# A new order of the start-up batch and of the unit stream in a fused attention and feed-forward kernel

## The chip, the cores and the metric

The kernel runs on one core of one Trainium2 chip. The metric is the device time in microseconds (us), taken as the median of several runs; most runs of a kernel agree within 0.3 us. Engines are named as the profile names them: PE is the matmul engine (TensorE), PEld its weight loads, DVE is VectorE, ACT is ScalarE, POOL is GpSimd, SP is SyncE. The profiled run also has a *span*, from its first to its last instruction, which is some 1.7 us shorter than the time of the same run.

## The reference

```python
# q, k, v: (8 batches, 8 heads, 576 positions, 64)
rel = pos[:, None] - pos[None, :]
mask_local   = (rel >= 0) & (rel < 32)                                 # heads 0..3
mask_strided = (rel >= 0) & (pos[None, :] % 32 == pos[:, None] % 32)   # heads 4..7
scores = where(mask, q @ k.T / sqrt(64), -1e9)
attn   = exp(scores - max) / (sum(exp(...)) + 1e-09)
x      = (attn @ v) as (8*576, 512)          # 4608 tokens
out    = relu(x @ w_in)**2 @ w_out           # 512 -> 2048 -> 512
```

## The kernel before

The attention is cut into *units*: unit u is batch u // 4 and head pair u % 4. Pairs 0 and 1 are local, pairs 2 and 3 strided. A unit goes through `step_T` (q or k transposed on PE into a PSUM bank, copied out by ACT for q and by DVE for k), `step_S` (scores on PE, exponentials on ACT, mask on DVE), `step_D` (outputs on PE, division by the row sum on DVE) and `step_E` (outputs transposed into `xt`, the input of the feed-forward part). Batch 0 has nothing to run beside and is written out by hand in `first_steps`; its strided units have `step_TS` for the transposes and `step_N`, `step_O` for row sums and outputs. The units from 8 on are spread between the feed-forward matmuls by `stream_steps` and `plan`.

The kernel takes eight PSUM banks (two, one and five), handed out in rotation from three lists:

```python
banks = {nm: [psum.tile([128, 512], FP32, name=f"{nm}{i}") for i in range(n)]
         for nm, n in (("ph", 2), ("py", 1), ("pt", 5))}
...
def step_T(u, name):
    ...
    pt = bank("ph" if u < 4 else "pt").bitcast(BF16)[:, 0:S]
    ...
    if name == "q":
        nc.scalar.copy(o, i)            # ACT
    else:
        nc.vector.tensor_copy(o, i)     # DVE
...
def step_TS(b, name, half, copy):       # header shortened here
    pt = bank("ph" if b == 0 else "pt").bitcast(BF16)[:, 0:S]
```

A *first-layer group* is 512 tokens by 128 of the 2048 columns: four matmuls of 512 columns, one for each head pair. Token chunk 0 lies within batch 0, so its groups can be fed piece by piece as each pair's `xt` comes in. `NP` groups are held open at once for that. Groups 0 and 1 take the two ph banks, group 2 the py bank, and groups from 3 on take pt banks *out of the rotation* until they are done:

```python
NP = 5
...
def part(kks, ffs=range(NP)):           # one of the four matmuls of each open group
    for ff in ffs:
        mm1(0, ff, kks, first_order, None if ff < 2 else "py" if ff == 2 else "pt")
...
order = [..., (o(2), 0), (lambda: part((a,)), 0), (E_(1), 0), (o(3), 0), (lambda: part((b,)), 0),
         (lambda: part((c,)), 0), (lambda: part((d,)), 0)]
# mm1: pool "pt" -> banks["pt"].pop(0); after the relu: banks["pt"].append(ph)
```

The number beside each step is how many filler matmuls follow it. They use no data; they keep PE busy while it would wait (18 matmuls of 512 columns in the profile, 7.5 us of its busy time). The constants (masks, and biases that add a large negative number to masked scores of batch 0) are built on DVE ahead of the first steps.

The softmax here doesn't subtract the row's maximum and nothing guards it: scores larger than these inputs give would overflow.

## Time and profile before

| | before |
|---|---|
| time, median of 3 runs | 310.63 us (310.61 to 311.06) |
| span of the profiled run | 309.1 us |
| PE busy | 301.5 us, 98% |
| PE busy in the first 20 us | 17.36 of 20 |
| PE busy in 70 to 80 us | 8.88 of 10 |
| mean granted clock | 1.00 |

PE is busy 98% of the time, so there is little to win: only the few stretches in which it is not full, or in which its instructions are stretched by short waits. A matmul of 512 columns stands in the trace as 0.379 us long, and the next one starts 0.216 after it (median of 985 such pairs in a row), so some 0.16 of a wait can pass without a gap (an estimate from these two figures). The prediction below shows the lines for this: the busy times, the stretches, and PE's waits. In a line of a timeline the columns are the start, the duration, the engine, the source line, the operation with output and input, their shapes, and how many instructions are joined in the line; in brackets is the idle time before it and what ended it.

### The profile page before, as it was taken

Reading aid. Unit: us, or ns where it says so; the run is one execution under the profiler, and the core shown is the slowest. Engines: PE = TensorE matmul, PEld = TensorE weight load, DVE = VectorE, ACT = ScalarE, POOL = GpSimd, SP = SyncE. Lnnn points to the kernel's source line nnn. Section 1 sums busy time; section 2 is a strip of 40 time slices with the busy share of each in tenths; the row PEclk is TensorE's granted clock in tenths of the full one; section 3 lists DMA queues with packets and bytes.
Section 4 is the critical chain, followed back from the end, with each engine's and each line's share of the span. In section 5 each row is a group of like instructions: output and inputs, shape, how many; then the busy total and the mean of one; then the engine's idle time right before and its main releaser. Section 6 shows DMA issues by size and latency. Waiting matters only on the chain.

```text
span 309.1 us, 6113 instructions
## 1 busy us (share of the span) xinstructions
PE 301.5 (98%) x2370; PEld 149.6 (48%) x2370; DVE 157.5 (51%) x408; ACT 165.0 (53%) x342; POOL 75.4 (24%) x103
## 2 busy tenths in 40 slices
PE   8999999998999999999999999999999999999995
PEld 3554564544554554445444544444444444444444
DVE  5366654578677884675566577445422222222200
ACT  3767737786566765554555655555444434344311
POOL 8653300540981045350461042000000000000000
PEclk9999999999999999999999999999999999999999
DMA  8999996997999899897999483221231000000121
GB/s 162 166 193 205 191 210 119 221 176 147 141 195 174 168 229 204 164 230 174 182 232 215 105 171 92 72 55 53 72 98 44 35 34 36 34 34 36 41 95 69
DMA packets 94119, 40.75 MB, mean 132 GB/s; under 512 B 78859, under 2 KB 87755, under 8 KB 93899
## 3 DMA queue, kind: packets, MB, share of 16 engines
q0 software_dynamic: 34528, 15.00, 39.1%
q1 hardware_dynamic: 59562, 25.37, 34.3%
q8 instruction: 18, 0.29, 0.4%
q14 instruction: 11, 0.08, 0.1%
HBM read 37.64 MB, written 13.57 MB: 166 GB/s over the span
## 4 chain that ended last, share of the span: by engine, by line
PE 93%; DVE 3%; ACT 1%; POOL 1%; issue 1%; ACTq 0%; POOLq 0%
PE ph L482 39%; PE py L518 28%; PE ph L518 9%; PE pt L337 4%; PE pt L422 4%; PE pt L482 1%; PE pt L288 1%; PE pt L518 1%; PE ph L504 1%; PE pt L458 1%; DVE kTl L303 1%; PE pt L325 1%; PE pt L398 1%; DVE x_l L435 1%; DVE x_s L435 1%
## 5 line engine op out<-in xcount | busy, mean ns | idle before, releaser
L482 PE MATMUL ph<-xt,w_in_b 128*128 128x512 bf16 x552 | 139.9, 379 | 0.0
L488 ACT ACTIVATE r<-ph 128x512 bf16<-128x512 f32 x138 | 82.4, 598 | 95.3 <-PE ph L482 93.0
L491 DVE TENSOR_TENSOR g_sb<-r 128x512 bf16<-128x512 bf16 x144 | 65.1, 453 | 105.8 <-ACT r L488 104.6
L518 PE MATMUL py<-w_out_b,g_sb 128*128 128x512 bf16 x400 | 102.8, 379 | 0.0
L482 PEld LDWEIGHTS <-w_in_b 128*128 128x128 bf16 x576 | 52.3, 98 | 55.3 <-issue 0.2
L518 PEld LDWEIGHTS <-g_sb 128*128 128x128 bf16 x560 | 50.8, 98 | 54.7 <-issue 0.4
L347 ACT ACTIVATE e<-pt 72x288 bf16<-72x288 f32 (+1 forms) x128 | 45.4, 407 | 12.7 <-PE pt L337 12.7
L518 PE MATMUL ph<-w_out_b,g_sb 128*128 128x512 bf16 x144 | 35.1, 379 | 0.0
L422 PEld LDWEIGHTS <-e 128*128 128x128 bf16 (+1 forms) x384 | 20.3, 97 | 15.3 <-issue 0.6
L435 DVE TENSOR_TENSOR x_s<-pt,rinv 72x384 bf16<-72x384 f32 (+1 forms) x36 | 18.3, 509 | 1.2
L434 DVE RECIPROCAL rinv<-pt 96x6 f32<-96x6 f32 (+2 forms) x68 | 12.6, 185 | 11.5 <-PE pt L422 11.1
L522 ACT COPY y<-py 128x512 f32<-128x512 f32 x25 | 14.6, 586 | 7.0 <-PE py L518 7.0
L435 DVE TENSOR_TENSOR x_l<-pt,rinv 96x384 bf16<-96x384 f32 x32 | 17.7, 554 | 1.1
L353 DVE TENSOR_TENSOR e<-e,mask_str 72x576 bf16<-72x576 bf16 x28 | 13.1, 482 | 3.8 <-ACT e L347 3.7
L353 DVE TENSOR_TENSOR e<-e,mask_full 128x576 bf16<-128x576 bf16 x28 | 12.6, 449 | 2.4 <-ACT e L347 2.2
L220 POOL CAST vl<-vl_st 128x768 bf16<-128x768 f32 x6 | 5.7, 951 | 32.7 <-DMA vl_st<-in_v_dram 20.1
L422 PE MATMUL pt<-vs,e 72*128 72x65 bf16 x192 | 11.9, 193 | 0.8 <-DVE e L353 0.4
L140 POOL CAST q_l<-q_st 96x768 bf16<-96x768 f32 x6 | 5.4, 900 | 25.9 <-DVE x_l L435 15.6
L522 ACT COPY y<-ph 128x512 f32<-128x512 f32 x9 | 5.3, 584 | 10.9 <-PE ph L518 10.9
L422 PE MATMUL pt<-vl,e 128*128 128x65 bf16 x192 | 10.9, 193 | 0.0
L612 POOL DMA_DIRECT2D vs<-in_v_dram x12 | 9.8, 819 | 0.2 <-issue 0.2
L337 PEld LDWEIGHTS <-kT_s 64*72 64x72 bf16 x256 | 5.9, 113 | 7.0 <-issue 6.2
(104 smaller groups left out, 197.5 us busy)
## 6 DMA issues: line engine op xcount, KB each, us to landing
out_dram<-y SPq DMA_DIRECT2D x35, 256.0 KB, 2.6
w_out_b<-in_moe_w_out_dram POOLq DMA_DIRECT2D x4, 512.0 KB, 15.4
q_d<-in_q_dram POOLq DMA_DIRECT2D x6, 288.0 KB, 7.4
k_d<-in_k_dram POOLq DMA_DIRECT2D x6, 288.0 KB, 8.5
q_st<-in_q_dram SPq DMA_DIRECT2D x12, 144.0 KB, 4.7
k_st<-in_k_dram SPq DMA_DIRECT2D x12, 144.0 KB, 4.5
vl_st<-in_v_dram SPq DMA_DIRECT2D x12, 144.0 KB, 4.1
v_st<-in_v_dram SPq DMA_DIRECT2D x6, 288.0 KB
```

The lines of the kernel that those rows point to most:

```text
L337: nc.tensor.matmul(pss[row][half][0:kn, w * i:w * (i + 1)], lhsT, rhs, start=u > 3, stop=True, skip_group_check=u < 4)
L347: nc.scalar.activation(e[0:kn, lo:lo + S // 2], pss[row][half][0:kn, 0:S // 2], AF.Exp, scale=scale)
L353: nc.vector.tensor_tensor(x, x, m, op=ALU.mult)
L422: nc.tensor.matmul(po[:, n - n0, :], e[0:kn, pos(n):pos(n) + 128], rhs[0:kn, src(n), 0:D + 1], start=True, stop=True)
L434: nc.vector.reciprocal(rinv[0:w, 0:m], po[0:w, 0:m, D:D + 1])
L435: nc.vector.tensor_tensor(x, po[0:w, 0:m, 0:D], rinv[0:w, 0:m].to_broadcast([w, m, D]), op=ALU.mult)
L482: nc.tensor.matmul(ph, w_in_b[:, kk, 128 * ff:128 * (ff + 1)], xt[kk][:, 512 * c:512 * (c + 1)], start=(kk == order[0]), stop=(kk == order ...
L488: nc.scalar.activation(r, ph, AF.Relu)
L491: later(1, lambda: nc.vector.tensor_tensor(g[:, ff, :], r, r, op=ALU.mult))
L518: nc.tensor.matmul(py, g[:, ff, 128 * j:128 * (j + 1)], w_out_b[:, ff, :], start=(ff == 0), stop=(ff == 15))
L522: nc.scalar.copy(y, py)
L612: nc.gpsimd.dma_start(out=t[:, NJ * i:NJ * (i + 1), 0:D], in_=v[b, h + i].rearrange("(p j) d -> p j d", j=NJ))
```

## The change

The intent is to take waits from PE in two places. In batch 0 the scores of unit 1 come before the strided transposes and unit 0's outputs before unit 3's scores, six groups are open instead of five, and two mask constants are built after the first casts. In the stream, k is transposed a step earlier than q instead of after it, and each unit's q and k are cast to bf16 as a pair, which takes k's cast a group earlier, and both casts of batch 4 a group earlier still. The q casts of batches 3 and 4 go to ACT.

```diff
-    NP = 5
+    NP = 6
...
         order = [(t(0, "q"), 2), (t(0, "k"), 2), (cast1("q"), 0), (cast1("k"), 0), (S_(0), 0),
-                 (t(1, "q"), 0), (t(1, "k"), 1), (ts("q", 0, v_), 0), (ts("q", 1, v_), 0), (S_(1), 1),
-                 (ts("k", 0, v_), 0), (ts("k", 1, s_), 1), (S_(2), 0), (S_(3), 0),
-                 (D_(0, 0), 0), (D_(0, 1), 1), (n(2), 1), (E_(0), 0), (D_(1, 0), 1), (n(3), 0), (D_(1, 1), 0),
+                 (t(1, "q"), 0), (t(1, "k"), 1), (S_(1), 0), (ts("q", 0, v_), 0), (ts("q", 1, v_), 1),
+                 (ts("k", 0, v_), 0), (ts("k", 1, s_), 1), (S_(2), 0), (D_(0, 0), 0), (D_(0, 1), 0), (S_(3), 0),
+                 (n(2), 1), (D_(1, 0), 0), (E_(0), 0), (n(3), 0), (D_(1, 1), 0),
                  (o(2), 0), (lambda: part((a,)), 0), (E_(1), 0), (o(3), 0), (lambda: part((b,)), 0),
...                                                   # stream_steps, per unit u
             if u < hi:
                 order.append(D_(u, 0))
+                if more:                              # u + 2 is local and has transposes on PE
+                    order.append(T_(u + 2, "k"))
             if u > lo:
                 order.append(E_(u - 1))
             if u < hi:
-                if u + 2 < hi and has_T(u + 2):
+                if more:
                     order.append(T_(u + 2, "q"))
                 order.append(D_(u, 1))
-                if u + 2 < hi and has_T(u + 2):
-                    order.append(T_(u + 2, "k"))
...                                                   # constants
+    cast_qk_local(0, (nc.scalar.copy, nc.vector.tensor_copy))      # (this line stood here before)
     nc.vector.tensor_copy(mask_full, ...)             # these three moved from ahead of the
     nc.vector.memset(mask_full[0:32, 0], 0.0)         # casts of unit 0 to behind them
     nc.vector.tensor_scalar(bias_s, ...)
...                                                   # plan
-                at(g1 + 2 * i, lambda u=4 * b + i: cast_qk_local(u, dve2, "q"))
-                at(g1 + 2 * i + 1, lambda u=4 * b + i: cast_qk_local(u, dve2, "k"))
+                copies = dve2 if b == 2 else (nc.scalar.copy, nc.vector.tensor_copy)
+                at(g1 + 2 * i, lambda u=4 * b + i, c=copies: cast_qk_local(u, c))
-    plan(4, 64, 62)
+    plan(4, 64, 61)
```

More of the change, by code (lines that the diff above doesn't have):

```diff
@@ L568, in stream_steps @@
         for u in range(lo, hi + 1):
+            more = u + 2 < hi and has_T(u + 2)
             if u < hi - 1:
@@ L663 @@
     nc.vector.memset(bias_l[0:32, 0, 0], -NEG)
-    nc.vector.tensor_copy(mask_full, mask_loc.to_broadcast([128, NL, QL]))
-    nc.vector.memset(mask_full[0:32, 0], 0.0)
-    nc.vector.tensor_scalar(bias_s, mask_str.to_broadcast([SP_, NJ // 2, SP_]),
-                            NEG, -NEG, op0=ALU.mult, op1=ALU.add)
     load_qk_str(0, "k", room=w_out_b[:, 4:10, :])
@@ L686 @@
     cast_qk_local(0, (nc.scalar.copy, nc.vector.tensor_copy))
+    nc.vector.tensor_copy(mask_full, mask_loc.to_broadcast([128, NL, QL]))
+    nc.vector.memset(mask_full[0:32, 0], 0.0)
+    nc.vector.tensor_scalar(bias_s, mask_str.to_broadcast([SP_, NJ // 2, SP_]),
+                            NEG, -NEG, op0=ALU.mult, op1=ALU.add)
     for fn, spare in first:
```

## The prediction

> **What bounds the kernel now.** I read the page's busy times and chain first, then stretches of 10 us, then what TensorE (PE) waited for, and last the order in time around each wait. From the page (busy times, then the chain that ended last):
>
> ```profile
> PE 301.5 (98%) x2370; PEld 149.6 (48%) x2370; DVE 157.5 (51%) x408; ACT 165.0 (53%) x342; POOL 75.4 (24%) x103
> ...
> PE 93%; DVE 3%; ACT 1%; POOL 1%; issue 1%; ACTq 0%; POOLq 0%
> ```
>
> PE is the bound nearly everywhere, so a reordering wins only what PE loses in waits. Where that is (stretch, its length, then busy us of PE, PEld, DVE, ACT, POOL):
>
> ```profile
> 0.00:10.00 10.00, 8.08 (x53) 3.39 (x54) 5.11 (x21) 4.56 (x8) 8.69 (x19) 1.00 0.94 157
> 10.00:20.00 10.00, 9.28 (x143) 5.58 (x143) 4.51 (x13) 8.00 (x21) 5.21 (x8) 1.00 1.37 181
> ...
> 70.00:80.00 10.00, 8.88 (x105) 4.97 (x101) 8.25 (x24) 5.36 (x14) 3.11 (x5) 1.00 0.63 114
> 80.00:90.00 10.00, 9.71 (x121) 5.60 (x121) 6.23 (x18) 5.97 (x16) 8.72 (x12) 1.00 1.70 199
> 90.00:100.00 10.00, 9.73 (x103) 5.03 (x102) 7.77 (x22) 6.19 (x15) 3.68 (x6) 1.00 1.83 178
> ```
>
> All other stretches of 20 to 300 us show PE full. So there are two places: the first 20 us (batch 0) and 70 to 95 us (the stream, units 10 to 16). The waits of PE, in order of time:
>
> ```profile
> 10.10 0.67 PE L189 MATMUL ph<-ident,w_out_b 96*128 96x96 bf16 x12 [0.52 <-ACT qT L301]
> 17.45 0.43 PE L458 MATMUL pt<-ident,x_l 96*128 96x96 bf16 x6 [0.55 <-DVE x_l L435]
> ...
> 74.89 0.22 PE L422 MATMUL pt<-vs,e 72*128 72x65 bf16 x2 [0.41 <-DVE x_l L435]
> 75.53 0.30 PE L422 MATMUL pt<-vs,e 72*128 72x65 bf16 x4 [0.42 <-DVE e L353]
> 79.54 0.43 PE L337 MATMUL pt<-qT,kTl 64*128 64x96 bf16 x12 [0.29 <-DVE kTl L303]
> 85.09 0.43 PE L337 MATMUL pt<-qT,kTl 64*128 64x96 bf16 x12 [0.29 <-DVE kTl L303]
> 93.27 0.43 PE L288 MATMUL pt<-ident,q_l 96*128 96x96 bf16 x6 [0.27 <-DVE q_l L140]
> ```
>
> [...] a "busy" PE hides waits of up to some 0.2 us; I therefore measure losses between starts. [...] in the trace the first-layer matmuls start at 19.24, 19.47, 19.69, 19.90, about 0.22 apart. [...] nothing of PE's starts between 74.01+0.47 and 74.89. [...]the trace shows 0.83 us for the one such cast on ACT (at 3.99), against 0.35 us for a bf16 one on DVE. I use 0.8.
>
> **The change, part by part.** All sums are between starts. The words "two PSUM banks for the last outputs" name nothing in the diff: the last outputs already alternate between the two ph banks, and I give that nothing.
>
> *Stream, 70 to 95 us.* What is lost now, against the same steps without a wait:
> - Scores of unit 12 (79.54) and 13 (85.09) come 0.58 after a four-matmul step that elsewhere takes 0.12 (106.09 to 106.21): 0.46 each. The cause is k's transpose coming right before: its DVE copy takes 0.74. The change puts k's transpose some 2 us earlier, so the copy is done. Gain 0.92. What is left is q's copy on ACT (0.64, possibly behind a 0.59 output copy); I have it end just when the scores come up, so 0 to 0.1 lost again.
> - q's transpose of unit 16 (93.27) comes 1.30 after a four-matmul group that takes 0.87: 0.43, because the cast sat late in DVE's queue (92.87). The casts now come a group earlier, q's on ACT, and k's transpose, not q's, is first. Gain 0.43.
> - Scores of unit 11 plus the first outputs of unit 10 took 1.66 (74.01 to 75.67); the like pair at 88.78 took 0.59. Lost: 1.07. DVE had four casts of 0.35 in the 4 us before; two go to ACT. DVE then frees the bank near 74.5 instead of 74.84 and finishes the mask near 74.9 instead of 75.48. But two casts of 0.8 now stand between ACT's exponentials, the last of unit 10 ends near 74.3 instead of 73.39, and in the new bank rotation unit 11's scores want that bank: some 0.35 of new wait before 74.01+. I have the pair end near 75.1: gain 0.55.
>
> Sum: 0.92 + 0.43 + 0.55 = 1.9, less 0.15 for the small ACT waits: 1.75 gained.
>
> *Batch 0.* I carried the new order on by hand with the durations and latencies of the trace.
> - k's cast goes ahead of the mask constants on DVE: it can start at 5.25, not 5.83. Two warm-up matmuls of 0.42 hold PE to 6.18, so k's transpose moves from 6.43 to 6.18: gain 0.25 so far.
> - Unit 1's scores go ahead of the strided q's transposes. The latter waited at 9.20 to 10.10; now the scores wait for their own k copy, to 9.97 (before: scores from 10.95). ACT's exponentials start 1.0 earlier. But the four strided transposes now follow each other through two ph banks: q half 0 at 10.79, DVE copies of 0.46 and 0.38, then k half 1 not before 12.19, its copy on ACT 12.66 to 13.30, scores of unit 2 at 13.35 instead of 13.39. The gain is nearly gone.
> - Unit 0's outputs come before unit 3's scores (14.17 instead of 15.46), so the 0.55 wait at 17.45 goes. In exchange unit 3's second half waits for the bank of the first output (x_l done 15.41) and the row sums for the second (16.12). Together with two warm-ups fewer (0.43) the first part of the six groups starts near 19.0 instead of 19.24.
> - Six groups open leave two pt banks in rotation. Unit 1's transposed output takes pt0, unit 3's two halves pt1 and then pt0 again, so the second half must wait for ACT's copy out of pt0. Before, the three had three banks and PE ran through:
>
> ```profile
> 20.33 0.42 PE L458 MATMUL pt<-ident,x_l 96*128 96x96 bf16 x6
> 20.68 0.50 PEld L398 LDWEIGHTS <-g_sb 72*64 72x64 bf16 x16
> 20.68 0.62 PE L398 MATMUL pt<-e,g_sb 72*64 72x72 bf16 x16
> 20.79 0.64 ACT L464 COPY xt<-pt 128x576 bf16<-128x576 bf16 x1 [0.80 <-PE pt L458]
> ```
>
> The copy ends 21.43 - 20.33 = 1.10 after the transposes start; PE has 0.5 of work before the second half needs the bank. New wait: 0.6. After: first part 19.0 to 20.3 (six of 0.216), transposes 20.3, second half of unit 3 at 21.45, three more parts of 1.3 from 21.67 to 25.57. Before, the same six groups were done at 24.48 (five) + 0.86 = 25.34.
>
> So batch 0 costs 0.2 net: about 1.0 of waits and fillers removed, 1.2 of bank waits added. I trust this to 0.6 either way; ten small waits are in it.
>
> *Elsewhere.* Casting batch 2 in pairs on DVE and the shifted ph banks (first group of chunk 1 on the other bank) meet a PE without waits; nothing. The two kernels have the same matmuls but for two warm-ups, so PE's work is the same.
>
> Sum: -1.75 + 0.2 = -1.55 in the span; 310.63 - 1.55 = 309.1.
>
> **The rivals.**
> 1. *The bank wait of the six groups is worse, or its gain better.* For worse: two banks must serve three tiles, and each bank wait is ACT or DVE time on PE's path. Against: the sixth group's 0.22 is filler exactly where unit 1's copy is awaited. If the wait after the first part vanished, 308.5; if batch 0 lost 0.8 instead of 0.2, 309.7.
> 2. *ACT becomes the bound of 70 to 80 us.* For: the two casts are 1.6 us of new ACT work in some 4 us in which it already has 3.5 us to do, in order, and relus free the first-layer banks. Against: ACT is busy 5.36 of 10 there, with 0.98 idle just before unit 11's exponentials. If the whole 1.07 stayed, 309.1 + 0.55 = 309.7; if the casts also delayed the relus by 0.5, 310.2.
> 3. *Transfers take over.* A kernel that runs 1.5 us earlier meets loads that don't move. The v rows of batch 3 land at 83.91 and 84.34 and are used at 86.33; batch 0's v at 13.68, used at 15.46 before and at 14.17 by my reckoning; the four w_in parts land at 16.33 to 20.97, used from 19.0 to 24.3. All have at least 0.5 left. If one bound, it would give back up to 1: 310.1.
> 4. *Nothing moves*, the stream's gain being hidden by later waits. From 95 us on PE never waits, with the casts' chain gone from batch 5 on, so earlier work stays earlier unless transposing transfers bind. 310.6.
>
> **Range and chances.** The centre is 309.1. Batch 0 gives +-0.6, the stream +-0.6, later transfers up to +0.7, runs differ by 0.45 (310.61 to 311.06). That makes 308.1 to 310.4. Faster by 2% would take 6.2 us; the whole kernel has only some 2.4 us of waits in the stream and about as much again in batch 0 after the first load. Slower by 2% would take a new wait of a size that nothing here suggests. So 0.01 each, 0.98 within 2%.
>
> **What would show it.** After: no wait of PE on kTl at the two score groups near 79 and 84; none on q_l near 92; a wait of the scores of unit 11 on ACT's e near 74, with two casts among ACT's exponentials; a wait of PE on ACT's xt copy (L464) of about 0.6 between the first and second part of the six groups; the scores of unit 2 still near 13.4; the sixth group done near 25.6. Wrong would be: waits of PE on a transfer, batch 0 ending more than 0.8 away from that, or ACT's casts holding first-layer groups.

## The result, and the profile after

Beside each other on one chip, the kernel before took 310.93 us (median of 6 runs, 310.61 to 311.37) and the changed kernel 309.86 us (6 runs, 309.78 to 310.65). The ratio is 0.9968, with a 95% interval of 0.9954 to 0.9982. Here and below a ratio is the mean time of one kernel's fast runs over that of the other's of the same rounds, so it is not quite the ratio of the medians. The change is a gain of about 1.0 us. The spans of the profiled runs are 309.1 and 308.1.

The page of the changed kernel, busy times and the chain that ended last:

```profile
PE 300.7 (98%) x2368; PEld 149.9 (49%) x2368; DVE 157.0 (51%) x404; ACT 167.3 (54%) x346; POOL 75.3 (24%) x103
...
PE 91%; DVE 5%; ACT 2%; POOL 1%; issue 1%; ACTq 0%; POOLq 0%
```

Nothing has changed hands: PE is still the bound. The four instructions that ACT has more, and DVE less, are the casts that went there. The stretches of the changed kernel, with the same columns as in the prediction (the last three are PE's granted clock and two measures of the transfers):

```profile
0.00:10.00 10.00, 7.65 (x55) 3.32 (x55) 5.76 (x21) 4.59 (x8) 8.69 (x19) 1.00 1.00 162
10.00:20.00 10.00, 9.14 (x140) 5.70 (x141) 5.20 (x14) 7.70 (x21) 5.89 (x9) 1.00 1.34 190
20.00:30.00 10.00, 9.52 (x63) 4.61 (x62) 5.56 (x21) 5.86 (x12) 4.04 (x6) 1.00 1.26 205
...
70.00:80.00 10.00, 9.65 (x116) 5.54 (x116) 8.20 (x23) 7.43 (x19) 2.60 (x4) 1.00 0.59 120
...
90.00:100.00 10.00, 9.91 (x103) 5.25 (x102) 7.66 (x20) 7.57 (x17) 4.34 (x6) 1.00 1.72 155
```

The stream has filled up: 9.65 instead of 8.88 in 70 to 80 us, 9.91 instead of 9.73 in 90 to 100. The start has not. PE's 20 to 30 us, which were full before (10.00), now have a hole of 0.48 us, and 70 to 80 us still lacks 0.35.

**The stream.** PE's lines around the score steps of units 11 to 14, and two of DVE's, from the timeline of the changed kernel:

```profile
74.34 0.49 PE L337 MATMUL pt<-qT_s,kT_s 64*72 64x72 bf16 x16
75.04 0.67 PE L422 MATMUL pt<-vs,e 72*128 72x65 bf16 x6 [0.20 <-DVE x_l L435]
75.54 1.03 PE L518 MATMUL ph<-w_out_b,g_sb 128*128 128x512 bf16 x4
...
79.05 0.43 PE L337 MATMUL pt<-qT,kTl 64*128 64x96 bf16 x12
...
90.48 0.34 DVE L140 COPY k_l<-k_st 96x768 bf16<-96x768 bf16 x1
90.53 0.47 PE L337 MATMUL pt<-qT_s,kT_s 64*72 64x72 bf16 x16
90.75 0.45 DVE L353 TENSOR_TENSOR e<-e,mask_str 72x576 bf16<-72x576 bf16 x1
90.93 0.62 PE L422 MATMUL pt<-vs,e 72*128 72x65 bf16 x6
91.39 1.03 PE L518 MATMUL ph<-w_out_b,g_sb 128*128 128x512 bf16 x4
...
92.25 0.42 PE L288 MATMUL pt<-ident,k_l 96*128 96x96 bf16 x6
```

Subtract starts to read it, because a start of the next work counts every wait, shown or hidden. In the kernel before, the wait at 93.27 has a bracket of 0.27, and between starts it costs 0.43 (four matmuls before it take 1.30, elsewhere 0.87):

| part of the stream | before | after | difference |
|---|---|---|---|
| unit 11's scores to the end of unit 10's first outputs (74.34 to 75.54) | 1.66 | 1.20 | -0.46 |
| from there to unit 12's scores (75.54 to 79.05) | 3.87 | 3.51 | -0.36 |
| the same stretch before unit 13's scores, which start at 84.24 | 5.55 | 5.19 | -0.36 |
| four matmuls to unit 16's first transpose (91.39 to 92.25) | 1.30 | 0.86 | -0.44 |
| unit 15's scores and unit 14's outputs (90.53 to 91.39) | 0.59 | 0.86 | +0.27 |
| sum | | | -1.35 |

The first four are waits that the change removed: those on kTl at 79.54 and 85.09 and on q_l at 93.27 no longer stand in the trace. The last is a new one. PE's outputs at 90.93 need the mask that DVE applies at 90.75, and DVE now does the cast at 90.48 right before it. The line shows no bracket, since the wait lies inside the group of six: 0.62 long, where six such matmuls without a wait end within about 0.35.

**Batch 0.** Four lines at the start, from the timeline of the kernel before and then from that of the changed kernel:

```profile
5.17 0.47 DVE L664 COPY mask_full<-mask_loc 128x576 bf16<-128x576 bf16 x1
5.52 1.66 POOL L237 DMA_DIRECT2D vl<-in_v_dram  x1
5.83 0.55 DVE L140 CAST k_l<-k_st 96x768 bf16<-96x768 f32 x1
7.05 0.76 DVE L303 COPY kTl<-ph 128x576 bf16<-128x576 bf16 x1 [0.67 <-PE ph L288]
```

```profile
5.17 0.71 DVE L140 CAST k_l<-k_st 96x768 bf16<-96x768 f32 x1
5.52 1.21 POOL L237 DMA_DIRECT2D vl<-in_v_dram  x1
5.80 1.03 DVE L684 COPY mask_full<-mask_loc 128x576 bf16<-128x576 bf16 x1
7.02 0.75 DVE L303 COPY kTl<-ph 128x576 bf16<-128x576 bf16 x1
```

The cast of k moved forward, from 5.83 to 5.17, and the transposes that need it from 6.43 to 5.94. But the copy of the mask, now behind the cast, took 1.03 us instead of the 0.47 of before, and kTl's copy queues behind it on DVE. It begins at 7.02; before it began at 7.05. Then the end of batch 0, from the timeline:

```profile
20.39 0.42 PE L458 MATMUL pt<-ident,x_l 96*128 96x96 bf16 x6
20.75 0.32 PE L398 MATMUL pt<-e,g_sb 72*64 72x72 bf16 x8
...
21.54 0.32 PE L398 MATMUL pt<-e,g_sb 72*64 72x72 bf16 x8 [0.48 <-ACT xt L464]
21.80 0.61 PE L482 MATMUL ph<-xt,w_in_b 128*128 128x512 bf16 x2
```

Before, the sixteen matmuls of unit 3's output ran in one go from 20.68 and the second part of the groups began at 21.23, 0.90 after the transposes. Now the second eight wait for ACT to read unit 1's transposed output out of the bank that they need, and the second part begins 1.41 after the transposes. All six groups are done at 25.69; before they were done at 25.34.

So the change gave 1.36 in the stream and lost 0.35 in batch 0: together 1.0, which is the difference of the spans.

### The profile page after: what moved, and what is told of

Same layout as the page of the kernel before. It is cut to its first block, busy times and chain, and to the rows that moved or that the text cites.

```text
span 308.1 us, 6114 instructions
## 1 busy us (share of the span) xinstructions
PE 300.7 (98%) x2368; PEld 149.9 (49%) x2368; DVE 157.0 (51%) x404; ACT 167.3 (54%) x346; POOL 75.3 (24%) x103
## 4 chain that ended last, share of the span: by engine, by line
PE 91%; DVE 5%; ACT 2%; POOL 1%; issue 1%; ACTq 0%; POOLq 0%
PE ph L482 37%; PE py L518 28%; PE ph L518 9%; PE pt L337 4%; PE pt L422 4%; PE pt L482 2%; PE pt L288 1%; DVE x_l L435 1%; PE pt L518 1%; PE ph L504 1%; PE pt L458 1%; DVE e L353 1%; DVE g_sb L491 1%; DVE k_l L140 0%; DVE kTl L303 0%
## 5 line engine op out<-in xcount | busy, mean ns | idle before, releaser
L220 POOL CAST vl<-vl_st 128x768 bf16<-128x768 f32 x6 | 5.0, 828 | 37.5 <-PE ph L482 21.2
L140 POOL CAST q_l<-q_st 96x768 bf16<-96x768 f32 x6 | 6.6, 1107 | 19.0 <-ACT r L488 16.5
```

## The experiments

Account A, which the trace above tells, says three things. The stream's gain comes from k's earlier transposes together with the casts. Batch 0 loses to the sixth group's bank and gains nothing at its start, because the mask constants now stand where they hold kTl's copy. And each of these losses can be repaired alone. Against it stand three rivals: that a part of the difference is only scatter between runs, that the transfers of v would take back what is repaired, and, in the stream, that the casts alone or the order alone do everything.

The unit of account below is a *shift*: how much later ACT's relus and output copies start than the same ones of the kernel before, counted in order. Over 31 to 67 us it says what batch 0 gained or lost; the difference of the spans says what the whole did. All outputs were correct.

| run | median us | range | ratio to before, 95% | shift after batch 0 | span less 309.1 |
|---|---|---|---|---|---|
| the change, first time | 309.86 | 309.78 to 310.65 | 0.9968 [0.9954, 0.9982] | +0.33 | -1.02 |
| e11: the change again | 310.08 | 309.76 to 310.46 | 0.9981 [0.9969, 0.9993] | +0.55 | -0.35 |
| e1: batch 0's part alone | 311.32 | 311.31 to 311.49 | 1.0022 [1.0005, 1.0039] | +0.31 | +0.31 |
| e2: the stream's part alone | 309.27 | 309.25 to 309.57 | 0.9956 [0.9942, 0.9971] | -0.14 | -1.51 |
| e3: five groups | 309.19 | 309.07 to 309.71 | 0.9955 [0.9940, 0.9970] | -0.34 | -1.06 |
| e4: second part as filler | 309.16 | 309.06 to 309.41 | 0.9952 [0.9937, 0.9967] | -0.33 | -1.68 |
| e5: mask constants later | 309.20 | 309.13 to 312.17 | 0.9983 [0.9932, 1.0033] | -0.18 | -1.53 |
| e6: strided k through pt | 309.58 | 309.35 to 309.64 | 0.9963 [0.9946, 0.9979] | -0.09 | -1.20 |
| e7: casts on DVE | 310.79 | 310.71 to 310.90 | 1.0003 [0.9988, 1.0018] | +0.34 | -0.23 |
| e8: old order of the stream | 310.51 | 310.47 to 310.59 | 0.9994 [0.9979, 1.0009] | +0.34 | -0.31 |
| e9: e4, e5 and e6 | 309.14 | 308.05 to 311.85 | 0.9976 [0.9939, 1.0013] | -0.80 | -2.04 |
| e10: e9, v not held back | 310.22 | 308.49 to 316.38 | 0.9972 [0.9935, 1.0010] | -1.25 | -2.29 |
| e12: e4 and e6 | 308.81 | 308.69 to 311.70 | 0.9958 [0.9929, 0.9986] | -0.76 | -2.11 |

The medians of before in these jobs were 310.70, 310.73, 310.62 and 310.65. Four runs each stand behind e1 to e8, six behind e9, e10 and e12, five behind e11.

### e1 and e2: each half of the change alone

e1 is the kernel before with `NP = 6`, the new `first_steps` and the moved constants. e2 is the kernel before with the new `stream_steps` and casts:

```diff
 # e1                                   # e2
-    NP = 5                             +                if more:
+    NP = 6                             +                    order.append(T_(u + 2, "k"))
 (order, constants: as in the change)    (casts, plan(4, 64, 61): as in the change)
```

> The kernel before with only the batch-0 half of the change (order, six groups, mask constants moved); stream and casts as before. Theory (the halves simply add; batch 0 costs what its six groups finish later, 25.69 against 25.34 us): span 309.1 + 0.35 = 309.4 us, slower than before, with the five waits of the stream near 74.9, 75.5, 79.5, 85.1 and 93.3 back, each about 0.3 us later. Rival (batch 0 is neutral or a gain that the stream half hides): span 308.7 to 309.1 us.

> The kernel before with only the stream half (k's transpose first, casts of batches 3 and 4 split over ACT and DVE and a group earlier); batch 0 as before with five groups. Theory (halves add): span 309.1 - 1.35 = 307.7 us, 0.4 us below the changed kernel, ratio to before near 0.9955. Rival (the stream's gain needs the batch-0 half, whose bank rotation and timing it was set for): span 308.1 us or more.

e1 took 311.32 us, 0.62 more than before. Of that some 0.2 lies outside the span (time less span is 1.9 in its four runs, 1.7 in those of before), and no run explains it. Its shift is +0.31 after batch 0 and still +0.31 at the end: what batch 0 loses is carried unchanged to the end of the kernel, and the waits on kTl and q_l stand in its stream as they did. e2 took 309.27, 1.43 less. Of its 1.51 of span 0.14 were there already after batch 0, whose code is that of before, so that is scatter; the stream gave 1.36 or 1.37, as in the changed kernel.

The halves add: +0.62 - 1.43 = -0.81, between the two measurements of the whole (-1.07 and -0.54). The batch-0 half of the change is a loss by itself, and the stream half alone is faster than before and than the whole change.

### e3: the changed kernel with five groups

```diff
-    NP = 6
+    NP = 5
```

> The changed kernel with NP = 5 instead of 6, nothing else, so that a third pt bank is left in rotation. Theory (the wait of 0.48 us for ACT's copy out of pt0 before the second half of unit 3's outputs is the price of the sixth group): that wait is gone, span 308.1 - 0.45 = 307.65 us. Rival (the sixth group's matmuls fill a wait that comes back without them): another wait of 0.2 to 0.5 us appears between 19 and 24 us and the span is 307.9 to 308.2 us.

e3 took 309.19. The timeline at the place of the bank wait:

```profile
20.19 0.42 PE L458 MATMUL pt<-ident,x_l 96*128 96x96 bf16 x6
20.54 0.45 PE L398 MATMUL pt<-e,g_sb 72*64 72x72 bf16 x16
```

The sixteen run in one go again: with three pt banks left in rotation the wait of 0.48 is gone. The shift after batch 0 falls from +0.33 to -0.34, by 0.67. So the sixth group costs more than the bracket of 0.48 says, and nothing that it gives in return is to be seen.

In the profiled run the gain did not reach the end, and the line that took it is a transfer's:

```profile
85.49 0.31 PE L422 MATMUL pt<-vl,e 128*128 128x65 bf16 x5 [0.48 <-DMA vl<-in_v_dram]
```

Unit 12's outputs waited for the v rows of batch 3, which landed at 85.44. In the changed kernel they land at 83.9 and 84.5 and are used at 85.48. It cost 0.64: the stream gave 0.72 here (1.06 less 0.34) instead of 1.36. This run took 309.71; the other three took 309.07 to 309.30, so they probably had less of this wait or none, though no profile of them was kept. The rival of the transfers is real, but it is seen in this one run alone.

### e4: six groups, the second part before unit 3's output

```diff
-                 (o(2), 0), (lambda: part((a,)), 0), (E_(1), 0), (o(3), 0), (lambda: part((b,)), 0),
+                 (o(2), 0), (lambda: part((a,)), 0), (E_(1), 0), (lambda: part((b,)), 0), (o(3), 0),
```

> The changed kernel, six groups, but the second part of the six groups (1.3 us of matmuls on xt2) is issued between unit 1's transposes and unit 3's outputs. Theory (the wait is for a bank that ACT is copying out of, so any ready work in front of it hides it): the 0.48 us wait is gone, span 307.6 to 307.7 us. Rival (unit 3's output, now 1.1 us later, becomes the wait of the fourth part, which reads xt3): PE waits 0.3 us or more on DVE's xt multiply near 23.7 us and the span is 307.9 us or more.

e4 took 309.16. The same place in its timeline:

```profile
20.66 0.38 PE L482 MATMUL ph<-xt,w_in_b 128*128 128x512 bf16 x1
...
22.05 0.45 PE L398 MATMUL pt<-e,g_sb 72*64 72x72 bf16 x16
```

The bank wait is filled with 1.3 us of work that does not need the bank, and the shift is -0.33. e3 and e4 remove the wait in different ways, one by a bank and one by order, and each is worth 0.66. This settles that the wait for the bank is the cost, not the sixth group's matmuls.

### e5: the two mask constants issued later

```diff
...                 # the three lines behind the casts of unit 0 are taken out
+    for i, (fn, spare) in enumerate(first):
+        if i == 4:      # just before unit 0's scores
+            nc.vector.tensor_scalar(bias_s, ...)
+        if i == 8:      # after unit 1's scores
+            nc.vector.tensor_copy(mask_full, ...)
+            nc.vector.memset(mask_full[0:32, 0], 0.0)
```

> The changed kernel with the mask constants of DVE moved again: the 0.18 us one to just before unit 0's scores, the 0.47 us one (needed only near 36 us) to after unit 1's scores. Theory (between k's cast and k's kTl copy the constants are in the way: the changed kernel's copy of mask_full took 1.03 us there and kTl's copy began at 7.02, as late as before): kTl's copy starts near 6.45, unit 0's scores near 7.3 instead of 7.83; at most 0.3 of the 0.5 us reaches the end of batch 0, because unit 0's outputs then meet the landing of v (14.07): span 307.6 to 307.85 us. Rival (something else sets kTl's copy, or the strided chain through two ph banks swallows it): scores of unit 2 still at 13.3 us or later and span 308.0 us or more.

The timeline of DVE in e5:

```profile
6.50 0.76 DVE L303 COPY kTl<-ph 128x576 bf16<-128x576 bf16 x1 [0.63 <-PE ph L288]
...
9.53 0.45 DVE L689 COPY mask_full<-mask_loc 128x576 bf16<-128x576 bf16 x1
```

kTl's copy begins at 6.50 instead of 7.02, and now it waits for PE rather than for DVE's own queue. Unit 0's scores follow at 7.32 instead of 7.83, and the shift after batch 0 goes from +0.33 to -0.18: 0.51. The earlier k cast is worth that only once the constants are out of its way. The mask's copy took 0.45 here. In the changed kernel and in all eight other profiles that have it right behind the cast, beside POOL's issue of v's load, it took 1.03. In e5 POOL issues loads of w_in beside it, one of them from 9.27 to 9.85, and the copy ends at 9.98; the part on the prediction comes back to this.

The expectation that v's landing (14.07 in the changed kernel) would let at most 0.3 of the gain through did not come about: v landed at 12.70 here, and unit 0's outputs began at 13.87. The landing scatters by itself, from 12.87 to 14.61 in the changed kernel, e3, e4, e7, e8 and e11, which are alike until then.

The median of e5 is 309.20; its interval is wide because one run of four took 312.17, at a mean clock of 0.988 (see e9).

### e6: k's strided transposes through the pt banks

```diff
-        pt = bank("ph" if b == 0 else "pt").bitcast(BF16)[:, 0:S]
+        pt = bank("ph" if b == 0 and name == "q" else "pt").bitcast(BF16)[:, 0:S]
```

> The changed kernel with the strided k transposes of batch 0 in two pt banks instead of the two ph banks. Theory (four strided transposes in a row are paced by DVE emptying two banks: 11.00, 11.27, then 12.05 and 12.4): the k transposes follow at 11.7, ACT copies at 12.3 instead of 12.87 and unit 2's scores end their wait near 13.0 instead of 13.56; the landing of v (14.07) caps it at 0.3: span 307.7 to 307.9 us. Rival (the pt banks are the scarce ones: the later waits for x_l and for ACT's copies stay where they are in time): span 308.1 us, or more.

In the changed kernel the four strided transposes of batch 0 start at 11.00, 11.27, 12.05 and about 12.4, the third and fourth waiting for the two ph banks of the first two. In e6 the third and fourth run in one go from 11.75, and unit 0's outputs at 13.96 instead of 14.37. The first part of the groups begins at 18.68 instead of 19.09, and the shift falls by 0.42. The whole 0.42 came through, as v had landed at 13.26. The median is 309.58, and the slowest of the four runs (309.64) is faster than the fastest of the eleven of the changed kernel (309.76). The two-bank chain that the prediction saw is a real cost, and it can be removed without the other repairs.

### e7 and e8: what the casts and the order in the stream are worth

e7 puts the four casts back on DVE and keeps the rest; e8 has the old `stream_steps` and keeps the new casts:

```diff
 # e7
-                copies = dve2 if b == 2 else (nc.scalar.copy, nc.vector.tensor_copy)
+                copies = dve2
 # e8
-                if more:
-                    order.append(T_(u + 2, "k"))     # after D_(u, 0)
+                if u + 2 < hi and has_T(u + 2):
+                    order.append(T_(u + 2, "k"))     # after D_(u, 1)
```

> The changed kernel with the q casts of batches 3 and 4 back on DVE, still in pairs and a group earlier. Theory (the two 0.35 us casts in front of unit 9's outputs and unit 10's mask are what ACT took over): scores of unit 11 plus first outputs of unit 10 take 0.25 to 0.35 us longer than the changed kernel's 1.20, the like pair near 90.5 also 0.3 longer, span 308.5 to 308.8 us. Rival (ACT's casts of 0.82 us are no help, as they delay unit 10's exponentials as much): span 307.9 to 308.2 us.

> The changed kernel with the stream's old order of transposes (q before k, k right before the scores) but with the split casts. Theory (k's early transpose alone removes the two waits for kTl): those waits are back near 79.1 and 84.6, 0.3 us each, span 308.1 + 0.7 = 308.8 us, and q's wait for its cast near 92.5 stays away. Rival (the casts moved off DVE let kTl's copy run early enough by themselves): waits under 0.15 us each, span 308.1 to 308.3 us.

e7 took 310.79, nearly 1.0 more than the changed kernel, and its span is 0.8 longer. From its table of PE's waits (engine and bank waited with, what ended it; then total, times, longest):

```profile
PE pt L422 <- DVE e L353: 0.7, 1, 0.7
PE pt L422 <- DVE x_l L435: 0.4, 1, 0.4
```

Both are waits of outputs on DVE. The one on x_l is at 75.25, where the changed kernel has 0.20, and the one on e is at 92.06, where unit 14's outputs wait for a mask that stands behind two casts instead of one. The pairs of scores and outputs take 0.20 and 0.59 longer from start to start. Together that is 0.79, which is the difference of the spans. The 0.59 is twice what was expected: the first of the two casts took 0.68 instead of 0.35, beside an issue of POOL (more on this under the prediction). Another 0.2 of e7's time lies outside the span, as in e1.

e8 took 310.51. Both waits on kTl are back, in its timeline of PE:

```profile
79.42 0.43 PE L337 MATMUL pt<-qT,kTl 64*128 64x96 bf16 x12 [0.30 <-DVE kTl L303]
...
84.98 0.43 PE L337 MATMUL pt<-qT,kTl 64*128 64x96 bf16 x12 [0.29 <-DVE kTl L303]
```

So the order removes the waits on kTl, and the q casts on ACT shorten those of the outputs. The wait on q_l at unit 16 stays away in both runs, so the earlier casts, which both have, are enough for it. Each half undone costs some 0.7 to 0.8 of the 1.36 in the stream. Neither does everything.

### e9, e10, e11, e12: the repairs together

e9 has the edits of e4, e5 and e6. e10 is e9 with the v rows of batch 3 no longer held back:

```diff
-    second(43, lambda: load_v_local_gated(3), rows(4), ...)
+    second(43, lambda: load_v_local_sw(3), rows(4), ...)
```

e11 is the changed kernel unedited, as a measure of scatter. e12 has the edits of e4 and e6, without e5's.

> The changed kernel with the three repairs of batch 0 together (second part of the six groups in front of unit 3's outputs; mask constants late; strided k transposes in pt banks). Theory A (the repairs remove waits that follow each other, so they add: 0.65 + 0.5 + 0.4): batch 0 ends 1.5 us earlier than in the changed kernel and the span is 306.5 to 306.7 us. Theory B (a program that runs this much earlier meets batch 3's v rows, which landed at 83.1 to 85.4 us in the runs so far, while unit 12's first outputs would now start near 83.9): batch 0 ends 1.3 to 1.5 us earlier, but PE waits 0.3 to 1.5 us for vl near 84, and the span is 307.0 to 308.0 us and spreads over the runs.

> As e9, but the load of batch 3's v rows no longer waits for a value of the batch's transposed k, so it is issued near 69 us, not 76. Theory B: the wait for vl near 84 is gone and the span is 306.5 to 306.8 us. Rival [...]: PE waits for kT_s at the scores of unit 14 near 87 us, span 307 us or more.

> The changed kernel itself, unedited, beside the two above on the same chip: median 309.8 +- 0.2 us, span 308.1 us, ratio to before 0.997; a control for the comparison.

> The changed kernel with two of the three repairs (second part of the six groups in front of unit 3's outputs; strided k transposes in pt banks), the mask constants left where the change put them. Theory (the late mask constants are what let the clock fall to 0.988 in 6 of the 16 runs of e5, e9 and e10, as no run of a kernel without them did): all runs at a clock of 0.998 or more, span 308.1 - 0.65 - 0.35 = 307.1 us, spread under 1 us. Rival (any program that is this early, or this chip's state, does it): one or more of the runs at 0.99 and some 3 us longer.

The spans of the profiled runs are the shortest of all: 307.0 for e9, 306.8 for e10, 307.0 for e12. The 306.5 to 306.7 of theory A was not reached. The repairs gave -1.13 (e9), -1.58 (e10) and -1.09 (e12) after batch 0 against the changed kernel's first run. Alone they gave 0.66, 0.51 and 0.42, together 1.59 for the three and 1.08 for e12's two. e12 adds up; e9 falls short by 0.46 and e10, which has the same batch 0, does not. The difference between these two is scatter of the start: k's first transposes took 0.69 us from 6.24 in e9 and 0.42 from 6.06 in e10. The first moment of full clock that the traces record was at 6.87 in e9 and 6.06 in e10, and anywhere from 3.96 to 6.87 in the thirteen profiles that record the clock (e4's does not; the kernel before has 6.78, the changed one 5.44). The changed kernel, e7, e8 and e11, which are the same up to the end of batch 0, have it from 3.96 to 5.51.

Holding the v rows back did no harm that the profiles show: they landed at 82.7 and 83.1 in e9, ahead of their use, and at 73.6 and 73.9 in e10. Nor did the early load of e10 show the harm of its rival: no wait of PE on kT_s stands in its table of waits, and its span is 306.8. Whether either does harm in the runs without a profile is not known.

e11 gives the scatter of the changed kernel itself: span 308.7 against 308.1. Of that 0.22 is in batch 0, and 0.33 in the pair that ends with unit 14's outputs (1.19 instead of 0.86), whose wait on the mask was 0.42 long here. The cast before that mask took 0.69 instead of 0.34: it began at 90.70, inside an issue of POOL from 90.39 to 91.23, while in the first profile POOL's issue began after it (90.61 against 90.48). A single profile of this kernel is good to some 0.7 us. The 0.66 of e3 and e4 is safer than that, because two kernels show it in their profiles and eight runs in their times.

Some runs of four kernels had a lower clock:

| kernel | runs at full clock | runs at mean clock 0.988 or 0.989 |
|---|---|---|
| e5 | 309.13 to 309.25 (3) | 312.17 |
| e9 | 308.05, 308.73, 308.94, 309.35 | 311.71, 311.85 |
| e10 | 308.49, 308.56, 308.79 | 311.65, 311.85, 316.38 |
| e12 | 308.69 to 309.52 (5) | 311.70 |

These are 7 of the 22 runs of these kernels. Each but the 316.38 costs about 3 us, more than all the repairs give. None of the 39 runs of the changed kernel and of the other experiments had it, nor any run of before: their means are 0.998 or more. The four have an early batch 0 in common, but e3, e4 and e6 are early too and show it in none of 12 runs. e12 was run to see whether e5's late constants are the cause. It does without them and has such a run too, so they are not needed for it. The traces record no lower grant than 0.5 (for 0.52 us after the end of the span in the kernel before, for 0.88 in the changed one); the low means are what 6.8 to 7.4 us at half the clock would give, which would cost 3.4 to 3.7 us of PE's work (an estimate from that grant, the means and the spans). No such run was profiled, so the cause stays open, and so does the 316.38, which is over 1.5% above the fastest run of its kernel and is left out of the ratio as slow. The other low-clock runs are in the ratios, which is why the intervals of e5, e9, e10 and e12 are wide.

So what would I use? e12 has the lowest median, 308.81. e4 and e3, at 309.16 and 309.19, are faster than both kernels too, and no low-clock run was seen in their four runs each. Four runs cannot exclude what one run in six shows in e12. On the evidence e12 is ahead by 0.35 us in the median, and level with e4 and e3 in the ratio to before, where its low-clock run counts: 0.9958 against 0.9952 and 0.9955.

## Why the prediction was right, and what was off in it

The time was predicted at 309.1 with a range of 308.1 to 310.4, and 309.86 was measured; against the kernel before of the same rounds the gain was 1.07, predicted 1.55. The difference of 0.5 is made up of 0.39 too much in the stream and 0.15 too little lost in batch 0. Step by step:

**The waits on kTl** (gain 0.92, less 0.15 for ACT). Right in kind and place; 0.72 was measured. e8 shows that the order is the cause. The 0.1 that is left at each is not the wait on q's copy that the prediction named: that copy ends at 78.85 and 84.05 on ACT, 0.2 before the scores. The same 0.1 stands before scores that wait for nothing. In the kernel before, the scores at 107.17 come 0.96 after the start of four matmuls that take 0.87 elsewhere. So the measure, 0.12 for a step with no scores behind it, was too small by 0.1, the two gains were 0.72 from the start, and the allowance of 0.15 nearly made up for it.

**q's transpose of unit 16** (gain 0.43). Right: 0.44.

**Unit 11's scores and unit 10's outputs** (gain 0.55). Nearly right, 0.46, but not by the predicted path, and so in part by luck. The wait of the scores on ACT's exponentials, foreseen at 0.35, did not come: the scores begin at 74.34, which is 74.01 plus batch 0's shift. On the other side DVE was done later than foreseen: x_l at 74.98 and the mask at 75.36, which is 0.15 and 0.13 after the predicted 74.5 and 74.9 moved by batch 0's 0.33. The pair still takes 0.61 longer than the 0.59 of one without waits, in a wait on x_l (0.20 in the bracket) and one on the mask inside the group of six.

**The term that was mis-sized in the stream** is the sum itself: "0.92 + 0.43 + 0.55 = 1.9, less 0.15" has no entry for the pair at 90.53. The prediction took the like pair of the kernel before (0.59) as the measure of a pair without waits and did not ask what the earlier casts would do to it. One cast of DVE lands before unit 14's mask there, and costs 0.27 (0.42 of wait in e11). The step was right about which work moves away, and omitted where it moves to.

**k's cast ahead of the constants** ("gain 0.25 so far"). This step failed. k's transposes did start earlier, by 0.49, but kTl's copy has to pass the constants on DVE, which the prediction does not mention. With the lengths of the kernel before they would have been done by 6.46 (5.25 + 0.55 for the cast + 0.66 for the constants), in time. One of them took 1.03 instead of 0.47, and unit 0's scores began at 7.83, against the 7.61 that the prediction implies and 7.86 before. These 0.22 are more than the 0.15 by which batch 0 missed. e5 shows that the constants are what held it, and that 0.51 was there to be had.

Why the copy took 1.03 is not shown as firmly. In thirteen of the fourteen profiles the copy of the mask ends 0.11 to 0.13 us after the end of the POOL issue in which it began. In the kernel before, that was the issue of k's load, from 4.81 to 5.53, and the copy ended at 5.64; in the changed kernel it was v's, from 5.52 to 6.72, and the copy ended at 6.83; in e5 it was w_in's, to 9.85, and it ended at 9.98. The copies of the thirteen began 0.26 to 0.36 us into their issues. In e9 it began 0.16 into an issue of 0.58 and was not held: it took 0.30, so the 0.47 and 0.45 are stretched too. The stretched casts of e7 and e11 end 0.15 to 0.16 after an issue in the same way. So the move put the copy beside a longer issue. Issues can be the longer ones too: that of v's load took 1.66 instead of 1.21 in the kernel before, where DVE's other constants and the cast of k ran beside it. What in an issue holds the copy, no run isolates. That it was stretched, and that its place held kTl, is shown.

**The strided chain** ("the gain is nearly gone", scores of unit 2 at 13.35). Right: they waited until 13.56. e6 shows that the two ph banks cause it and that it is worth 0.42.

**The bank wait of six groups** ("New wait: 0.6", second half of unit 3's output at 21.45, six groups done at 25.57). Right in place and size: 21.54 and 25.69, with 0.48 idle and 0.67 from start to start (unit 3's sixteen matmuls and the wait take 1.05, from 20.75 to 21.80, and in e4 they take 0.38, from 22.05 to 22.43). e3 and e4 confirm it twice.

**The rivals.** Rival 1 is what came about in small: batch 0 lost 0.33 to 0.35 instead of 0.2. Rival 2 did not: ACT holds no first-layer group, and putting its casts back on DVE (e7) makes things worse. Rival 3 did not in the changed kernel, but its margin is thin, as one run of e3 shows with 0.48. Rival 4 is excluded by e1 and e2, whose shifts are carried to the end.

## What to carry to other kernels

Where one engine is 98% busy, add up start-to-start losses for each wait that a reordering removes, and then do the same for the place where the moved work lands: the two terms that were off here are both work in the way of something else on DVE, once a cast before a mask and once a constant before a copy. A buffer held open was paid here by those who share the rotation: holding one more PSUM bank for a sixth group cost 0.66 us, and the same kernel with five groups, or with the next work put into the gap, was faster. Before keeping a change of two parts, run each alone: one half of this one was a loss of 0.6 us (0.3 in the span of its profile) inside a gain of 1.0.
